# Sliding-window attention and a channel mix on one core: the tails of q and k in one transposition, q's part moved inside SBUF, the softmax division in two steps, multiplications that either of two engines may do, and new orders on all five engines

## The chip, the core and the metric

The kernel runs on one core of a Trainium2 chip. The core has TensorE (PE in the profile; its weight loads stand apart as PEld), VectorE (DVE), ScalarE (ACT), GpSimd (POOL) and SyncE (SP), and 16 DMA engines that its queues share. POOL's queue loads from HBM and turns float32 into bfloat16 on the way; SP's queue stores the output, copies inside SBUF and transposes by DMA. The metric is the device time of one launch in microseconds, the median of several runs. Before the change it is 231.72 us (three runs, 230.85 to 231.91).

## The reference

Batch 8, 8 heads, 576 tokens, head dimension 64; the channel mix has model width 512 and inner width 1024.

```python
# attention: causal, a window of 128 tokens, a linear bias by head
scores = scale * np.matmul(q, k.transpose(0, 1, 3, 2))
mask = (rel >= 0) & (rel < window)
scores = np.where(mask, scores + bias[None], -1000000000.0)
attn = np.exp(scores - np.max(scores, axis=-1, keepdims=True))
attn = attn / (np.sum(attn, axis=-1, keepdims=True) + 1e-09)
x = heads_side_by_side(np.matmul(attn, v))            # (8, 576, 512)
# channel mix; x_prev is x one token earlier, zero before the first
xk = mu_k * x + (1.0 - mu_k) * x_prev
xr = mu_r * x + (1.0 - mu_r) * x_prev
k = np.maximum(xk @ w_k, 0.0)
out = 1.0 / (1.0 + np.exp(-(xr @ w_r))) * (k * k @ w_v)
```

The middle lines are shortened: `heads_side_by_side` stands for a transposition and a reshape.

## The kernel before

**Pairs and batches.** The work on attention goes by pairs of heads: pair `it` is batch `it // 4`, heads `2 * (it % 4)` and the next, 32 pairs in all. Within a pair the 576 tokens are four blocks of 128 and a tail of 64. For the channel mix two batches make one group P of 1152 rows, four groups in all; a group's rows are cut into column chunks (`c0` is a chunk's first row), and its output into nine blocks of 128 rows.

**Steps and their names.** Every step has a name, and the engines' orders are lists of these names. For a pair: `tr` turns q and k of two pairs from "token by dimension" to "dimension by token" on VectorE (line 180; batches 0 and 1 do it on TensorE instead, `tq`, `tk`, and copy the result out of PSUM with `pq`, `pk`). `sh` copies the turned q inside SBUF, shifted by 32 partitions (line 196, SP's queue), because the scores read q of the next block at the same partitions as k. `score` multiplies k and q (lines 242 and 247; 229 in batches 0 and 1), `exp` is the exponential on ScalarE (line 263), `mask` multiplies by the banded bias on VectorE (line 271), `av` multiplies by v (line 287; a column of ones beside v gives the softmax's denominator), `norm` takes the reciprocal of that column (line 297) and multiplies by it (line 298), `ot` and `xt` transpose the result so that the model dimension lies on the partitions (TensorE and ScalarE, lines 306 and 317; from batch 4 on one DMA transposition on SP's queue, line 311). `dl` is x minus the token before (line 330), `ma` multiplies that by mu_k and by mu_r (line 336, two instructions), `xk` adds the token before (line 347). In batch 0 these steps come in two halves, columns 0 to 255 and 256 to 575.

For a group: `m1` is xk times w_k for one of eight slices of the inner width (line 359), `rl` the relu out of PSUM (ScalarE, line 365), `kk` its square (ScalarE, line 372, or VectorE, line 374: whichever list names it), `m3` is xr times w_r (line 381), `rs` its tanh (line 387), `m2a` and `m2` are the squares times w_v (line 396), `oo` joins both into the output (VectorE, line 402) and `st` stores it (SP's queue, line 408). `fill` are matrix products of zeros that TensorE does between other work in the first 31 us.

**The tails of q and k.** The last 64 tokens of a batch's q and k come by two loads on POOL's queue, `lts` (line 118; 64 KB each), each into partitions 64 to 95 of its half of a buffer that the turned tail of k later overwrites in part. `turn_tail` (line 188, steps `tl.b.0` and `tl.b.1`) then turns each with a VectorE operation of 32 partitions, into partitions 96 to 127, for batches 2 to 7: twelve operations. A batch's scores wait for both.

**Buffers.** Tiles of one kind rotate: four for the relu's output, three for the output, three for x's differences (`dl`), three for the scaled differences (`mb`), two PSUM tiles for scores and `av`, four PSUM banks for everything else.

**Order.** Five strings, one for each engine, fix the order of the steps on that engine word for word; an engine does them in that order and waits at each for what the step needs. The loop `plan` only interleaves the five lists and hands out rotating buffers in that order. SP's list mixes `sh`, `xt` and `st`: a step whose data are late holds up those behind it.

Of the kernel before, what the change touches and what calls it, by code (L numbers as in the profile page):

```python
# [16 lines left out]
def kernel(  # L17
# [12 lines left out]
    nc = tc.nc  # L30
# [29 lines left out]
    rlp = ctx.enter_context(tc.tile_pool(name="rlp", bufs=4))  # L60
    otp = ctx.enter_context(tc.tile_pool(name="otp", bufs=3))
# [15 lines left out]
    tl_buf = [kl.rearrange("p h c t -> p (h c t)").rearrange("p (i h c) -> p i h c", i=2, h=H)  # L77
              for kl in kl_buf]
# [9 lines left out]
    dl_buf = [cst.tile([128, S], BF16, name=f"dl{i}") for i in range(3)]  # L88
    mb_buf = [cst.tile([128, 2, S], BF16, name=f"mb{i}") for i in range(NMB)]
# [22 lines left out]
    def load_tail(b, i):  # L112
# [4 lines left out]
        else:  # L117
            nc.gpsimd.dma_start(
                out=tl_buf[b % 2][64:96, i],
# [65 lines left out]
    def turn_tail(b, i):  # L185
        dst = (words(kl_buf[b % 2], 128)[96:128, :, 0:64] if i else
               words(q2_buf[b % 2], 256)[96:128, :, 128:192])
        nc.vector.transpose(
            dst.rearrange("p h (c r) -> p h r c", r=2),
            tl_buf[b % 2][64:96, i].rearrange("p h c -> p (h c)").bitcast(FP32).rearrange(  # L190
                "p (h r d) -> p h r d", r=2, d=32))

# [98 lines left out]

    def norm(it, t0, t1):
        n = t1 - t0
        a5 = T.pop(("av", it, t0))[:, :, 0:n * W].rearrange("p h (t c) -> p h t c", c=W)
        rc = xup.tile([128, 2, NJ], FP32, tag="rc", name="rc")
        xu = T["xu", it, t0] = xup.tile([128, NJ, 2, D], BF16, tag="xu", name="xu")
        nc.vector.reciprocal(out=rc[:, :, 0:n], in_=a5[:, :, :, D])
        nc.vector.tensor_tensor(  # L298
            out=xu[:, t0:t1].rearrange("p t h d -> p h t d"), in0=a5[:, :, :, 0:D],
            in1=rc[:, :, 0:n, None].to_broadcast([128, 2, n, D]), op=ALU.mult)  # L300
# [28 lines left out]
    def delta(it, c0=0, c1=S):  # L329
        nc.vector.tensor_tensor(out=ring_of("dl", dl_buf, it, c0)[:, c0:c1], in0=x_of(it, c0, c1),  # L330
                                in1=x_of(it, c0 - 1, c1 - 1), op=ALU.subtract)

    def scaled(it, c0=0, c1=S):
        mb, g = ring_of("mb", mb_buf, it, c0), it % G
        for w in range(2):
            nc.vector.tensor_scalar(out=mb[:, w, c0:c1], in0=T["dl", it][:, c0:c1],  # L336
# [681 lines left out]
```

## Time and profile before

| | us |
|---|---|
| median of three runs | 231.72 |
| profiled execution | 231.78 |
| its span in the profile | 229.9 |
| TensorE busy in the span | 218.2 |
| VectorE busy | 190.4 |
| ScalarE busy | 172.7 |
| GpSimd busy | 76.4 |

The span runs from the first to the last instruction; 1.9 us of the profiled execution lie outside it. The granted TensorE clock was 1.00 in every stretch. A row of the groups by form names line, engine, operation, output and inputs, partitions by elements, count, then busy time in all and the mean duration of one in ns, then the idle time just before them. A row of the waits names who waited for whom, the total, how many times and the longest. A row of the stretches gives, for each engine, its busy time within the stretch.

### The profile page before, as it was taken

The page shows a single profiled execution, that of the slowest core. Times are in us where ns is not written, and L with a number is a line of the kernel's source. Part 1 is how long each engine was busy: PE and PEld are TensorE (multiplying, and loading weights), DVE is VectorE, ACT ScalarE, POOL GpSimd, SP SyncE. Part 2 cuts the span into 40 slices and gives each one's busy share as a digit, 9 for nine tenths or more (in the row PEclk, how much of TensorE's full clock was granted, in tenths as well). Part 3 has the DMA queues.
Part 4 walks back from the last instruction along what each step waited for, and adds up shares of the span by engine and source line. Part 5 has one row for each costly group of instructions (what it writes and reads, how often), then busy time and mean ns, then how long its engine had stood idle before and what let it go on. Part 6 is the DMA issues. An engine that isn't in the chain of part 4 may idle for free.

```text
span 229.9 us, 5654 instructions
## 1 busy us (share of the span) xinstructions
PE 218.2 (95%) x2226; PEld 128.1 (56%) x2261; DVE 190.4 (83%) x397; ACT 172.7 (75%) x326; POOL 76.4 (33%) x118
## 2 busy tenths in 40 slices
PE   7789989998999999999999999999999999999993
PEld 3446648755766555655566655556565465456541
DVE  7239999999899999999999999999989984761132
ACT  3968999996898997895699896868588668038810
POOL 8989864436565753271139100000000000000000
PEclk9999999999999999999999999999999999999999
DMA  5999999999999999999969996153422124240023
GB/s 112 164 145 157 175 157 201 209 172 182 228 199 185 182 210 199 155 134 208 114 128 112 220 141 146 33 165 128 91 80 74 48 56 120 99 152 26 0 98 130
DMA packets 83225, 31.82 MB, mean 138 GB/s; under 512 B 55032, under 2 KB 78592, under 8 KB 83200
## 3 DMA queue, kind: packets, MB, share of 16 engines
q0 software_dynamic: 61904, 16.52, 79.9%
q1 hardware_dynamic: 21296, 14.95, 25.8%
q8 instruction: 17, 0.28, 0.5%
q14 instruction: 8, 0.07, 0.1%
HBM read 33.56 MB, written 9.44 MB: 187 GB/s over the span
## 4 chain that ended last, share of the span: by engine, by line
PE 74%; DMA 10%; DVE 8%; POOL 3%; issue 1%; ACT 1%; SPq 1%; DVEq 0%; POOLq 0%
PE ps L359 25%; PE pv L396 22%; PE pr L381 11%; PE sa L287 6%; PE sa L242 4%; DMA qt<-qt 4%; DMA out_dram<-ot 3%; DMA vs<-in_v_dram 3%; DVE mb L336 2%; PE xp L306 1%; DVE xm L347 1%; PE sa L229 1%; DVE dl L330 1%; DVE xu L298 1%; PE sa L217 1%
## 5 line engine op out<-in xcount | busy, mean ns | idle before, releaser
L263 ACT ACTIVATE at<-sa 128x1024 bf16<-128x1024 f32 x64 | 64.0, 1031 | 13.7 <-PE sa L247 10.0
L359 PE MATMUL ps<-xm,wk_sb 128*128 128x256 bf16 (+2 forms) x412 | 70.4, 313 | 0.9 <-DVE xm L347 0.6
L396 PE MATMUL pv<-wv_sb,kk 128*128 128x512 bf16 x274 | 66.6, 379 | 0.8 <-issue 0.3
L365 ACT ACTIVATE rl<-ps 128x256 bf16<-128x256 f32 (+2 forms) x104 | 46.1, 474 | 14.0 <-PE ps L359 13.2
L359 PEld LDWEIGHTS <-wk_sb 128*128 128x128 bf16 x416 | 38.9, 98 | 22.5 <-issue 0.2
L396 PEld LDWEIGHTS <-kk 128*128 128x128 bf16 x288 | 26.9, 98 | 28.7
L372 ACT ACTIVATE kk<-rl 128x256 bf16<-128x256 bf16 (+2 forms) x79 | 38.4, 512 | 0.3
L271 DVE TENSOR_TENSOR at<-at,mask 128x1024 bf16<-128x1024 bf16 x56 | 36.9, 680 | 0.9 <-ACT at L263 0.8
L402 DVE SCALAR_TENSOR_TENSOR ot<-rs,pv 128x512 f32<-128x512 bf16 x36 | 24.4, 681 | 14.4 <-PE pv L396 10.5
L381 PE MATMUL pr<-wr_sb,xm 128*128 128x512 bf16 x131 | 35.2, 379 | 0.7
L99 POOL DMA_DIRECT2D vs<-in_v_dram x32 | 28.6, 902 | 20.1 <-PE sa L287 11.1
L387 ACT ACTIVATE rs<-pr 128x512 bf16<-128x512 f32 x36 | 21.3, 605 | 17.3 <-PE pr L381 17.1
L287 PEld LDWEIGHTS <-at 128*128 128x128 bf16 x576 | 21.6, 98 | 6.5 <-issue 1.0
L347 DVE TENSOR_TENSOR xm<-mb,xt 128x1152 bf16<-128x1152 bf16 (+3 forms) x40 | 24.4, 631 | 0.1
L298 DVE TENSOR_TENSOR xu<-sa,rc 128x640 bf16<-128x640 f32 x28 | 23.1, 824 | 1.0
L336 DVE TENSOR_SCALAR mb<-dl,mu_sb 128x576 bf16<-128x576 bf16 (+2 forms) x72 | 23.5, 386 | 0.2
L381 PEld LDWEIGHTS <-xm 128*128 128x128 bf16 x144 | 13.3, 98 | 12.3
L287 PE MATMUL sa<-vs,at 128*128 128x65 bf16 x448 | 18.8, 194 | 0.0
L242 PE MATMUL sa<-qt,kt 32*128 32x256 bf16 (+1 forms) x384 | 15.7, 266 | 1.2 <-DMA qt<-qt 0.7
L124 POOL DMA_DIRECT2D ql<-in_k_dram x15 | 11.7, 778 | 14.7 <-DVE kt L180 9.7
L374 DVE TENSOR_TENSOR kk<-rl 128x256 bf16<-128x256 bf16 (+2 forms) x25 | 8.0, 330 | 8.1 <-ACT rl L365 8.1
L330 DVE TENSOR_TENSOR dl<-xt 128x576 bf16<-128x576 bf16 (+2 forms) x36 | 14.6, 415 | 0.0
(72 smaller groups left out, 208.9 us busy)
## 6 DMA issues: line engine op xcount, KB each, us to landing
out_dram<-ot SPq DMA_DIRECT2D x36, 256.0 KB, 2.5
vs<-in_v_dram POOLq DMA_DIRECT2D x32, 128.0 KB, 8.3
ql<-in_k_dram POOLq DMA_DIRECT2D x15, 256.0 KB, 7.3
ql<-in_q_dram POOLq DMA_DIRECT2D x15, 256.0 KB, 7.6
qt<-qt SPq DMA_DIRECT2D x12, 192.0 KB, 6.8
wk_sb<-in_moe_w_k_dram POOLq DMA_DIRECT2D x2, 512.0 KB, 7.9
wv_sb<-in_moe_w_v_dram POOLq DMA_DIRECT2D x2, 512.0 KB, 13.2
tv<-in_v_dram POOLq DMA_DIRECT2D x8, 64.0 KB, 7.8
```

Source lines behind the costliest of these rows:

```text
L99: nc.gpsimd.dma_start(out=vs_buf[b % NLD][:, j, :, 0:D], in_=v[b, :, 128 * j:128 * j + 128, :].rearrange("h p d -> p h d"))
L263: nc.scalar.activation(out=to, in_=sa, func=AF.Exp, scale=float(scale))
L271: nc.vector.tensor_tensor(out=a, in0=a, in1=m, op=ALU.mult)
L287: nc.tensor.matmul(pa[:, hl, W * (t - t0):W * (t - t0) + W], lhsT=at[:, lo:lo + 128], rhs=vs[:, u, 2 * g + hl, :] if u < NF else tvb[:, 2 ...
L298: nc.vector.tensor_tensor(out=xu[:, t0:t1].rearrange("p t h d -> p h t d"), in0=a5[:, :, :, 0:D], in1=rc[:, :, 0:n, None].to_broadcast([12 ...
L336: nc.vector.tensor_scalar(out=mb[:, w, c0:c1], in0=T["dl", it][:, c0:c1], scalar1=mu_sb[:, NPO * w + g:NPO * w + g + 1], scalar2=None, op0 ...
L347: nc.vector.tensor_tensor(out=xm_buf[P % 2][:, w0:w1, o:o + c1 - c0], in0=T["mb", it][:, w0:w1, c0:c1], in1=x_of(it, c0 - 1, c1 - 1)[:, No ...
L359: nc.tensor.matmul(ps[:, 0:c1 - c0], lhsT=wk_sb[:, po, 128 * fo:128 * fo + 128], rhs=xk[:, po, c0:c1], start=(po == 0), stop=(po == NPO - 1))
L365: nc.scalar.activation(out=rl[:, 0:c1 - c0], in_=T.pop(("ps", P, c0, fo))[:, 0:c1 - c0], func=AF.Relu, scale=RELU_SCALE)
L372: nc.scalar.activation(out=out_, in_=in_, func=AF.Square)
L381: nc.tensor.matmul(pr, lhsT=T["xr", P][:, po, 128 * c:128 * c + 128], rhs=wr_sb[:, po], start=(po == 0), stop=(po == NPO - 1))
L396: nc.tensor.matmul(pv, lhsT=kk[:, fo, o:o + 128], rhs=wv_sb[:, fo], start=(fo == 0), stop=(fo == NFO - 1))
```

## The change

Six things change, and with them the order of the steps on every engine.

- **Tails.** Both loads go to one buffer, q in partitions 0 to 31 and k in 32 to 63, and one VectorE operation of 64 partitions turns both into partitions 64 to 127 (step `tl.b`, six operations instead of twelve). k's part lies there where the scores read it. q's part is copied from there by a new DMA on SP's queue, step `mt.b` (32 partitions of 8 times 256 bytes, 64 KB), and the scores wait for that copy.
- **Division.** `norm` is split in two steps with the same two instructions: `rc` (reciprocal) and `norm` (multiplication), so that other VectorE steps may stand between them.
- **Multiplications by mu.** `ma` and the new `mr` are the products with mu_k and mu_r, each a step of its own, and each may be on VectorE or on ScalarE, as the lists name them. 39 stand on VectorE and 29 on ScalarE (before: 72 on VectorE; in batch 0 the product with mu_r is no longer cut in halves). The difference, both products and their buffer are one rotating tile of three now, where there were three for differences and three for products.
- **Buffers.** Four for the output instead of three, three for the relu's output instead of four.
- **Squares and copies.** 45 of the 104 squares stand on VectorE instead of 25, and five of the eight copies `pk` instead of two.
- **Orders.** All five strings are new. TensorE has the same steps as before, the 14 `fill` among them.

```diff
-    rlp = ctx.enter_context(tc.tile_pool(name="rlp", bufs=4))
-    otp = ctx.enter_context(tc.tile_pool(name="otp", bufs=3))
+    rlp = ctx.enter_context(tc.tile_pool(name="rlp", bufs=3))
+    otp = ctx.enter_context(tc.tile_pool(name="otp", bufs=4))
...
-    tl_buf = [kl.rearrange("p h c t -> p (h c t)").rearrange("p (i h c) -> p i h c", i=2, h=H)
-              for kl in kl_buf]
+    tl_buf = [kl.rearrange("p h c t -> p (h c t)")[0:64, 0:1024].rearrange(
+        "p (h c) -> p h c", h=H) for kl in kl_buf]
...
-    dl_buf = [cst.tile([128, S], BF16, name=f"dl{i}") for i in range(3)]
-    mb_buf = [cst.tile([128, 2, S], BF16, name=f"mb{i}") for i in range(NMB)]
+    mb_buf = [cst.tile([128, 3, S], BF16, name=f"mb{i}") for i in range(NMB)]
...
-                out=tl_buf[b % 2][64:96, i],
+                out=tl_buf[b % 2][32 * i:32 * i + 32],
...
-    def turn_tail(b, i):
-        dst = (words(kl_buf[b % 2], 128)[96:128, :, 0:64] if i else
-               words(q2_buf[b % 2], 256)[96:128, :, 128:192])
+    def turn_tail(b):
         nc.vector.transpose(
-            dst.rearrange("p h (c r) -> p h r c", r=2),
-            tl_buf[b % 2][64:96, i].rearrange("p h c -> p (h c)").bitcast(FP32).rearrange(
+            words(kl_buf[b % 2], 128)[64:128, :, 0:64].rearrange("p h (c r) -> p h r c", r=2),
+            tl_buf[b % 2].rearrange("p h c -> p (h c)").bitcast(FP32).rearrange(
                 "p (h r d) -> p h r d", r=2, d=32))
+
+    def move_tail(b):
+        nc.sync.dma_start(out=words(q2_buf[b % 2], 256)[96:128, :, 128:192],
+                          in_=words(kl_buf[b % 2], 128)[64:96, :, 0:64])
...
+    def recip(it, t0, t1):
+        n = t1 - t0
+        a5 = T["av", it, t0] = T["av", it, t0][:, :, 0:n * W].rearrange(
+            "p h (t c) -> p h t c", c=W)
+        rc = T["rc", it, t0] = xup.tile([128, 2, NJ], FP32, tag="rc", name="rc")
+        T["xu", it, t0] = xup.tile([128, NJ, 2, D], BF16, tag="xu", name="xu")
+        nc.vector.reciprocal(out=rc[:, :, 0:n], in_=a5[:, :, :, D])
...
-    def scaled(it, c0=0, c1=S):
-        mb, g = ring_of("mb", mb_buf, it, c0), it % G
-        for w in range(2):
-            nc.vector.tensor_scalar(out=mb[:, w, c0:c1], in0=T["dl", it][:, c0:c1],
-                                    scalar1=mu_sb[:, NPO * w + g:NPO * w + g + 1], scalar2=None,
-                                    op0=ALU.mult)
+    def scaled(it, w, act, c0=0, c1=S):
+        mb, i = T["mb", it], NPO * w + it % G
+        mu = mu_sb[:, i:i + 1]
+        if act:
+            nc.scalar.activation(out=mb[:, w, c0:c1], in_=mb[:, 2, c0:c1], func=AF.Copy, scale=mu)
+        else:
+            nc.vector.tensor_scalar(out=mb[:, w, c0:c1], in0=mb[:, 2, c0:c1], scalar1=mu,
+                                    scalar2=None, op0=ALU.mult)
...
-            lq.0.0 lmu.0 lq.0.1 lmu.1 sh.2.0 sh.2.1 st.0.1 st.0.0 sh.3.0 st.0.2 sh.3.1
+            lq.0.0 lq.0.1 lmu.1 lmu.0 sh.2.0 mt.2 sh.2.1 mt.3 sh.3.0 sh.3.1 st.0.1 mt.4
...
-                for i in range(2):
-                    op(("tl", b, i), "DVE", 600, lambda i=i: turn_tail(b, i),
-                       [("lts", b, i)] + ([("clear",)] if i else []) + war, n)
+                op(("tl", b), "DVE", 640, lambda: turn_tail(b),
+                   [("lts", b, 0), ("lts", b, 1), ("clear",)] + war, n)
+                op(("mt", b), "SP", 60, lambda: move_tail(b), [("tl", b)], n, dma=300)
...
-            ready = [("tr", b, g // 2, 1), ("sh", b, g // 2), ("tl", b, 0), ("tl", b, 1)]
+            ready = [("tr", b, g // 2, 1), ("sh", b, g // 2), ("mt", b)]
```

Three places of the new orders follow, as the built programs have them. A row names line, operation, output and inputs, and the size of the output; the number after a name tells which buffer it is, and equal neighbours are counted in one row. Line numbers after the change are a few higher: the transposition of q and k is line 180 before and 179 after, that of the tails 188 and 185.

The first place is VectorE while batch 2 gets ready, between the division of batch 1 and its last `xk`. `qt` and `kt` are the turned q and k, `kl` the buffer of the tails. Before:

```order
L180 STREAM_TRANSPOSE kt_85<-ql_79 128x4x4x32
L297 RECIPROCAL rc<-sa 128x10
L298 TENSOR_TENSOR xu<-sa,rc 128x2x5x64
L330 TENSOR_TENSOR dl_99<-xt_95 128x576
L330 TENSOR_TENSOR dl_100<-xt_95 128x576
L336 TENSOR_SCALAR mb_102<-dl_99,mu_sb 128x576 x2
L330 TENSOR_TENSOR dl_98<-xt_95 128x576
L188 STREAM_TRANSPOSE kl_87<-kl_87 32x8x2x32
L347 TENSOR_TENSOR xm_96<-mb_102,xt_95 128x2x576
L374 TENSOR_TENSOR kk<-rl 128x256
L336 TENSOR_SCALAR mb_103<-dl_100,mu_sb 128x576 x2
L180 STREAM_TRANSPOSE qt_89<-ql_79 128x4x4x32
```

After:

```order
L179 STREAM_TRANSPOSE kt_85<-ql_79 128x4x4x32
L346 TENSOR_SCALAR mb_99<-mb_99,mu_sb 128x576 x2
L179 STREAM_TRANSPOSE qt_89<-ql_79 128x4x4x32
L337 TENSOR_TENSOR mb_98<-xt_95 128x576
L346 TENSOR_SCALAR mb_100<-mb_100,mu_sb 128x576
```

Between the transposition of k (first row) and the second one of q stood twelve instructions, and now stand two; the tail of batch 2 was turned earlier, in one operation.

The second place is SP's queue from the first copy inside SBUF on, `qt<-qt` being the shifted copy, `qt<-kl` the new copy of q's tail and `out_dram<-ot` a store. Before:

```order
L196 DMA qt_89<-qt_89 96x4x128 x2
L408 DMA out_dram<-ot 128x512 x2
L196 DMA qt_90<-qt_90 96x4x128
L408 DMA out_dram<-ot 128x512
L196 DMA qt_90<-qt_90 96x4x128
```

After:

```order
L197 DMA qt_89<-qt_89 96x4x128
L191 DMA qt_89<-kl_87 32x8x64
L197 DMA qt_89<-qt_89 96x4x128
L191 DMA qt_90<-kl_88 32x8x64
L197 DMA qt_90<-qt_90 96x4x128 x2
L417 DMA out_dram<-ot 128x512
```

The copies of the tails of batches 2 and 3 stand ahead of later shifted copies, and the first store now stands behind both shifted copies of batch 3.

The third place is ScalarE in the second column chunk of group 2 (384 wide), where `at<-sa` is the exponential, `mb<-mb,mu_sb` the multiplication by mu, `rl<-ps` the relu, `kk<-rl` the square and `rs<-pr` the tanh. Before:

```order
L365 ACTIVATE rl<-ps 128x384
L372 ACTIVATE kk<-rl 128x384
L365 ACTIVATE rl<-ps 128x384
L263 ACTIVATE at_84<-sa 128x2x2x256
L365 ACTIVATE rl<-ps 128x384 x3
L387 ACTIVATE rs<-pr 128x512
L372 ACTIVATE kk<-rl 128x384
```

After:

```order
L374 ACTIVATE rl<-ps 128x384 x5
L344 ACTIVATE mb_99<-mb_99,mu_sb 128x576
L396 ACTIVATE rs<-pr 128x512
L264 ACTIVATE at_84<-sa 128x2x2x256 x2
L396 ACTIVATE rs<-pr 128x512
```

Five relus now stand in a row with three buffers for them, and their squares are VectorE's.

324 lines of the change are left out of this document (168 added, 156 removed).

## The prediction

> **What bounds the kernel now.** I read the page first, then the busy time by stretches, then the waits, then the stretches around TensorE's waits. The page:
>
> ```profile
> PE 218.2 (95%) x2226; PEld 128.1 (56%) x2261; DVE 190.4 (83%) x397; ACT 172.7 (75%) x326; POOL 76.4 (33%) x118
> PE   7789989998999999999999999999999999999993
> DVE  7239999999899999999999999999989984761132
> ACT  3968999996898997895699896868588668038810
> ```
>
> TensorE is busy nearly everywhere after the first slices, but VectorE is as full until three quarters of the span. The stretches say how much each has left (columns: stretch, its length, then busy time of PE, PEld, DVE, ACT, POOL):
>
> ```profile
> 0.00:31.30 31.30, 27.24 (x345) 15.32 (x350) 21.12 (x74) 24.97 (x43) 27.29 (x54) 1.00 1.76 148
> 31.30:60.00 28.70, 27.22 (x333) 19.48 (x335) 27.69 (x55) 25.64 (x56) 16.15 (x21) 1.00 1.65 199
> 60.00:108.00 48.00, 47.38 (x511) 27.09 (x517) 47.25 (x84) 41.94 (x75) 24.02 (x32) 1.00 1.58 183
> 108.00:112.00 4.00, 3.67 (x50) 2.14 (x48) 3.36 (x6) 1.55 (x3) 0.00 (x0) 1.00 1.04 188
> 112.00:180.00 68.00, 67.01 (x718) 39.65 (x728) 65.88 (x128) 55.47 (x103) 8.94 (x11) 1.00 0.73 114
> 180.00:226.00 46.00, 45.64 (x284) 24.46 (x287) 24.44 (x55) 23.12 (x51) 0.00 (x0) 1.00 0.24 81
> ```
>
> 31.3 us is where the channel mix begins on TensorE, 226 where TensorE ends; the last 3.9 us are the last product and store. From 31.3 to 226 TensorE idles 1.48 + 0.62 + 0.33 + 0.99 + 0.36 = 3.78 us. The change takes no work off TensorE. So what it can win is within these 3.78 us and the first 31.3, where TensorE idles 4.06. The waits:
>
> ```profile
> PE sa L242 <- DMA qt<-qt: 0.7, 1, 0.7
> PE ps L359 <- DVE xm L347: 0.6, 1, 0.6
> PE sa L242 <- DVE xu L298: 0.3, 1, 0.3
> ```
>
> These are TensorE's waits of a known cause from 31.3 us on. The second is the channel mix's first product, which waits for `xk`; the first and the third are one place each:
>
> ```profile
> 46.79 1.10 DVE L180 STREAM_TRANSPOSE qt<-ql 128x512 f32<-128x512 f32 x1
> 47.91 8.06 DMA qt<-qt
> 56.11 0.40 PE L242 MATMUL sa<-qt,kt 32*128 32x256 bf16 x8 [0.70 <-DMA qt<-qt]
> ```
>
> Scores of pair 10 wait for the shifted q, whose copy took 8.06 us from the end of its transposition.
>
> ```profile
> 101.72 7.91 DMA out_dram<-ot
> 108.63 0.69 DVE L402 SCALAR_TENSOR_TENSOR ot<-rs,pv 128x512 f32<-128x512 bf16 x1 [0.16 <-DMA out_dram<-ot]
> 109.71 0.69 DVE L402 SCALAR_TENSOR_TENSOR ot<-rs,pv 128x512 f32<-128x512 bf16 x1 [0.39 <-DMA out_dram<-ot]
> 111.44 0.41 PE L242 MATMUL sa<-qt,kt 32*128 32x256 bf16 x8 [0.33 <-DVE xu L298]
> ```
>
> Here two outputs wait until a store has left one of the three output tiles; the division of pair 16 stands behind them on VectorE, and the scores of pair 20 wait for it to free a PSUM tile.
>
> **The change part by part.** The prices:
>
> ```profile
> L188 DVE STREAM_TRANSPOSE qt<-kl 32x512 f32<-32x512 f32 x6 | 4.2, 706 | 0.2
> L188 DVE STREAM_TRANSPOSE kl<-kl 32x512 f32<-32x512 f32 x6 | 4.2, 706 | 0.2
> L180 DVE STREAM_TRANSPOSE qt<-ql 128x512 f32<-128x512 f32 x12 | 13.2, 1102 | 0.0
> L336 DVE TENSOR_SCALAR mb<-dl,mu_sb 128x576 bf16<-128x576 bf16 x56 | 18.8, 385 | 0.2
> L336 DVE TENSOR_SCALAR mb<-dl,mu_sb 128x320 bf16<-128x320 bf16 x8 | 2.6, 362 | 0.0
> L336 DVE TENSOR_SCALAR mb<-dl,mu_sb 128x256 bf16<-128x256 bf16 x8 | 2.3, 419 | 0.0
> L374 DVE TENSOR_TENSOR kk<-rl 128x256 bf16<-128x256 bf16 x12 | 3.4, 282 | 0.5 <-ACT rl L365 0.5
> L374 DVE TENSOR_TENSOR kk<-rl 128x384 bf16<-128x384 bf16 x9 | 3.1, 354 | 7.6 <-ACT rl L365 7.6
> L374 DVE TENSOR_TENSOR kk<-rl 128x512 bf16<-128x512 bf16 x4 | 1.7, 418 | 0.0
> L372 ACT ACTIVATE kk<-rl 128x256 bf16<-128x256 bf16 x36 | 14.3, 430 | 0.1
> L372 ACT ACTIVATE kk<-rl 128x384 bf16<-128x384 bf16 x23 | 12.0, 533 | 0.1
> L372 ACT ACTIVATE kk<-rl 128x512 bf16<-128x512 bf16 x20 | 12.3, 635 | 0.1
> L129 DVE COPY qt<-tp 128x512 bf16<-128x512 bf16 x2 | 1.4, 690 | 3.2 <-PE tp L149 1.7 <-PE tp L154 1.5
> L132 ACT COPY qt<-tp 128x512 bf16<-128x512 bf16 x14 | 7.5, 607 | 0.5 <-PE tp L154 0.5
> ```
>
> *Tails.* Twelve operations of 0.706 us go, six of 64 partitions come. No row shows 64 partitions; at an equal 512 columns it lies between 0.706 (32 partitions) and 1.102 (128). A third of the way, as 64 lies between 32 and 128, is 0.84. VectorE saves 8.5 - 5.0 = 3.4 us (1.9 to 4.2).
>
> *Multiplications.* Busy time per instruction is 18.8/56 = 0.336 us, in halves 0.325 and 0.29. On VectorE 35 whole ones and four halves remain: 13.0 us against 23.7, a saving of 10.7. ScalarE gets 25 whole ones and four halves. It has no such row; the squares of 256 and 512 columns put 576 at 0.69 (0.64 to 0.75 allowed), halves at 0.43 and 0.48: 25 x 0.69 + 1.8 = 19.1 us more.
>
> *Squares and copies.* The lists have 18, 17 and 10 squares of 256, 384 and 512 columns on VectorE against 12, 9 and 4, which is 15.3 - 8.2 = 7.1 us more there and 6 x 0.430 + 8 x 0.533 + 6 x 0.635 = 10.7 less on ScalarE. Three copies add 2.1 on VectorE, and take 1.8 from ScalarE.
>
> VectorE: -3.4 - 10.7 + 7.1 + 2.1 = -4.9, 190.4 to 185.5 us. ScalarE: +19.1 - 10.7 - 1.8 = +6.6, 172.7 to 179.3. Neither is the path as such; what counts is TensorE's waits.
>
> *Term 1, the shifted q of batch 2.* From the division of pair 2 to the transposition at 46.79, VectorE now does less: one tail operation less (1.41 to 0.84), the four halves that go to ScalarE, in both products (2.45), the other halves of mu_r against three whole ones (1.2 - 1.0), and `dl`, both products and `xk` of pair 5, which now stand behind (0.4 + 0.7 + 0.7); more by a copy of 0.7, a copy of the mask of about 0.6 and two squares of 0.28. That is some 3.2 us less. It begins later by 1 to 1.5, since the reciprocal of pair 2 now waits behind more exponentials. The copy should land some 2 us earlier, and the wait of 0.70 goes: **-0.7** (0 if all of it is lost again).
>
> *Term 2, the fourth output tile.* The output at 109.71 no longer needs the store that has just left: **-0.4** (0 to -0.6, as VectorE idles 0.16 + 0.39 there and TensorE 0.33).
>
> *Term 3, a lighter VectorE.* Of the 1.97 us that TensorE idles in 60 to 108 and 112 to 226 I give a quarter to the 4.9 us less and to the reciprocals that no longer hold their multiplications: **-0.5** (0 to -2.0).
>
> *Term 4, the first 31.3 us.* The order of TensorE there is another: all scores of batch 1 and two of its `av` now precede the channel mix, about 2.4 us of work that stood behind. So its begin may come 2.4 us later at no cost. For it: VectorE's relief of 3.2. Against it: a load on GpSimd now precedes the distances from which ScalarE's masks are made, the reciprocal that waits, and w_k's loads, issued behind five loads of v. These look to be of one size, and I take **0** (-1.5 to +1.5).
>
> *At nothing.* The new copies: six issues on SP's queue, which stands waiting for VectorE most of the time.
>
> ```profile
> SPq L196 <- DVE qt L180: 59.4, 8, 32.7
> SPq L408 <- DVE ot L402: 62.7, 16, 13.8
> DMA to landing us min/median/max: 2.7/6.8/8.1
> ```
>
> The last row is that of the shifted copies. In five of six batches the tail's copy is issued ahead of one of that batch's own shifted copies, three times its size (64 against 192 KB), so the scores wait for that one anyway; in batch 5 it is issued right behind them. If it took 8.1 us and the cover were gone, each batch would lose up to the 0.7 that pair 10 lost. What waits behind it on SP are stores, and they now have a fourth tile. The split of the division adds no instruction.
>
> Sum: 231.78 - 0.7 - 0.4 - 0.5 + 0 = 230.2 us for the profiled execution, which lies 0.06 above the median: **230.1 us**.
>
> **The rivals.**
>
> *ScalarE becomes the bound (slower).* Its stretches, same columns as above:
>
> ```profile
> 20.00:50.00 30.00, 28.69 (x391) 20.06 (x396) 29.47 (x80) 28.97 (x61) 18.44 (x25) 1.00 1.68 180
> 60.00:100.00 40.00, 39.53 (x442) 23.21 (x447) 39.36 (x68) 36.13 (x67) 21.12 (x28) 1.00 1.58 182
> ACT rl L365 <- DVE kk L374: 0.6, 2, 0.4
> ```
>
> In 20 to 50 us it has 1.03 left. The lists put six multiplications there (3.2 us) and take a copy and, on balance, a square away (1.0): 1.2 too much. In 60 to 100 twelve whole ones come (8.3) and seven squares go (3.9): 36.13 + 4.4 = 40.5 in 40, 0.5 too much. With three relu tiles a relu also waits for VectorE's squares, as twice before with four; 20 more squares there at a third of the 0.3 of such a wait make 2 us, of which I count half. If ScalarE sets the pace, terms 1 to 3 don't count: 231.8 + 1.2 + 0.5 + 1.0 = 234.5; with half the relu waits hidden, 233.5. It decides once ScalarE idles less than about 1 us in 20 to 50. Against it: VectorE was at 29.47 of 30 there and cost TensorE little. The Trainium skill (ScalarE: Activation LUTs, Rules for kernel authors) tells to put multiplications on VectorE rather than ScalarE, since VectorE is faster per element; the trace agrees, 0.336 against some 0.69 us, and by that rule this rival should hold. The skill's Perfetto Trace Analysis (Optimizing Scalar/DVE Operations) allows the move where VectorE is saturated, which 29.47 of 30 shows.
>
> *The first 31.3 us eat the gain (no change).* The reciprocal of pair 2 stands ahead of a copy, the division of pair 0's second half and all its differences. If it waits 1.5 us and nothing makes that good, 230.1 + 1.5 = 231.6.
>
> *VectorE was the true bound (faster still).* If its 3.2 us by 46.8 reach TensorE in part, -1.5 in the beginning, and all of term 3's range: 231.7 - 0.7 - 0.4 - 2.0 - 1.5 = 227.1.
>
> *The move costs what it saves.* A 64-partition transposition of 1.10 us saves 1.9 instead of 3.4, and a late copy of q's tail costs 0.7 in each of six batches: 230.1 + 4.2 = 234.3. SP's waits above speak against it.
>
> **How the numbers follow.** Forecast 0.42 (229.0 to 231.0; I count a seventh of it as no change), VectorE as true bound 0.14, no change 0.23, ScalarE as bound 0.16, the late tail 0.05. A measurement tells from no change what is beyond 0.5%, 1.16 us: faster is below 230.56, slower above 232.88. Faster: 0.36 + 0.14 = 0.50; same: 0.06 + 0.23 = 0.29; slower: 0.21. The range runs from 227.6, near the third rival's end, to 233.5, the milder form of the first; the forecast's own is 229.0 to 231.0.
>
> **What would show it.** Right: no wait of the scores for the shifted copy, none of the output for a store, VectorE near 185.5 us busy and idling before 100, ScalarE near 179, TensorE idling under 2.5 us after its first channel-mix product. Wrong: long waits of relus for squares or for `mb`, a first channel-mix product later than 31.3 + 2.4 + 1 us, scores that wait for `qt<-kl`, or a tail operation above 1 us.

## The result, and the profile after

The changed kernel takes **242.81 us** (median of four, 240.64 to 243.49) against 231.68 (four runs, 230.85 to 231.91): ratio **1.0478, 95% interval 1.0436 to 1.0519**. 230.1 was forecast. Its profiled execution took 243.2 us, its span is 241.4. Here and below a ratio leaves out executions more than 1.5% above the fastest of the same kernel, and the kernel before was timed anew with each group of runs, so a ratio need not equal the quotient of the medians beside it.

The page of the changed kernel, busy times first, then the span in 40 slices of 6 us:

```profile
PE 223.7 (93%) x2226; PEld 129.6 (54%) x2261; DVE 181.5 (75%) x381; ACT 181.3 (75%) x332; POOL 76.9 (32%) x118
...
PE   8989889999999999999949699999999999999992
...
DVE  5346999989999789899397587999999858224032
...
PEclk9999999999999999999997979999999999999999
```

VectorE is 8.9 us lighter than before and still the kernel is 11 us longer. Counted from 1, TensorE has holes in slices 21 and 23 and VectorE in slices 20 to 25, and the granted clock dips in slices 22 and 24. The stretches of the changed kernel (columns as in the prediction: stretch, length, PE, PEld, DVE, ACT, POOL, granted clock, DMA share, GB/s) place the loss:

```profile
0.00:31.30 31.30, 27.39 (x344) 15.23 (x349) 19.57 (x59) 25.15 (x41) 29.26 (x57) 1.00 1.68 145
31.30:60.00 28.70, 27.46 (x323) 19.37 (x329) 27.73 (x65) 26.78 (x63) 14.68 (x20) 1.00 1.52 194
60.00:108.00 48.00, 46.67 (x535) 27.29 (x542) 44.55 (x80) 45.29 (x76) 21.81 (x29) 1.00 1.60 180
...
112.00:145.00 33.00, 27.30 (x256) 14.29 (x252) 23.77 (x44) 21.68 (x35) 8.64 (x11) 0.90 1.35 133
145.00:180.00 35.00, 34.47 (x372) 20.38 (x377) 32.36 (x65) 28.68 (x50) 0.00 (x0) 1.00 0.45 90
```

The same stretch of the kernel before:

```profile
112.00:145.00 33.00, 32.58 (x365) 19.79 (x369) 32.62 (x62) 28.32 (x56) 8.94 (x11) 1.00 1.18 141
```

TensorE does 256 matmuls there instead of 365. It idles 33.00 - 27.30 = 5.7 us, where it idled 0.4 before; its granted clock is 0.90 instead of 1.00. To see how late it is at each moment, I gave every step of TensorE's list its lower-quartile time in the two traces compared, and asked how much later than in the kernel before the same sum of work begins. In the changed kernel this lateness is -0.4 us at 30 us, 0.4 at 60, 1.8 at 100, 1.3 at 120, 5.8 at 130, 9.5 at 140, 11.2 at 145 and 11.0 at the end. **Nearly 10 of the 11 us are lost between 120 and 145 us.** Below, three numbers (at 120, at 145, at the end) stand for this.

Who waits between 80 and 146 us in the changed kernel (total, times, longest):

```profile
POOL ql L123 <- DVE kt L179: 12.4, 1, 12.4
DVE mb L337 <- DMA xt<-xu: 8.2, 3, 3.7
...
PE sa L243 <- DVE xu L303: 4.6, 3, 2.3
```

VectorE stands for x's transposition by DMA (`dl` waits for `xt`), and TensorE's scores stand for VectorE's division, which frees a PSUM tile. The chain of waits of the changed kernel (start, us, what) shows how the one makes the other:

```profile
92.74 7.97 DMA ql<-in_q_dram
...
107.65 11.51 DMA xt<-xu
...
125.83 0.83 DVE xu L303
...
127.25 8.72 DMA xt<-xu
...
136.37 0.83 DVE xu L303
...
137.25 0.37 PE sa L243 x5
```

x of pair 16 takes 11.5 us from its issue to its use, x of pair 20 takes 8.7. VectorE's own rows there:

```profile
114.68 0.82 DVE L303 TENSOR_TENSOR xu<-sa,rc 128x640 bf16<-128x640 f32 x1
119.19 0.46 DVE L337 TENSOR_TENSOR mb<-xt 128x576 bf16<-128x576 bf16 x1 [3.68 <-DMA xt<-xu]
...
132.92 0.21 DVE L299 RECIPROCAL rc<-sa 128x10 f32<-128x10 f32 x1
136.00 0.46 DVE L337 TENSOR_TENSOR mb<-xt 128x576 bf16<-128x576 bf16 x1 [2.86 <-DMA xt<-xu]
136.37 0.82 DVE L303 TENSOR_TENSOR xu<-sa,rc 128x640 bf16<-128x640 f32 x1
```

The last three are the point: the new list has the differences of pair 20 between the reciprocal and the multiplication of pair 21's division, and the scores of pair 24 wait for that multiplication. In the list before, the order there is `norm.21 dl.20`. And SP's queue of the changed kernel, where each step waits for its data in order:

```profile
112.68 0.55 SPq L417 DMA_DIRECT2D out_dram<-ot  x1
122.35 0.62 SPq L191 DMA_DIRECT2D qt<-kl  x1
123.03 0.61 SPq L197 DMA_DIRECT2D qt<-qt  x1
123.69 2.31 SPq L317 DMA_TRANSPOSE xt<-xu  x1
```

x of pair 19, divided at 115.5, leaves only at 123.7, behind the tail's copy and the first shifted copy of batch 6. These wait for VectorE, which itself waited 3.7 us for x of pair 16.

What shares the DMA engines with the transpositions: the view of the transfers from 105 to 140 us (40 slices, then the share of GpSimd's queue, then the transpositions with their median landing), of the changed kernel

```profile
DMA  9769999999996999999999999999999999984094
...
q0 software_dynamic: 12560, 2.62, 90.7%
...
xt<-xu SPq DMA_TRANSPOSE x6, 5.8
```

and of the kernel before:

```profile
DMA  9999999329017999039999399999999999893702
...
q0 software_dynamic: 10829, 2.23, 76.2%
...
xt<-xu SPq DMA_TRANSPOSE x6, 4.0
```

Before, the engines are lightly used for some 5 us from 111 us on, when the first transpositions run (slices of 3, 2, 9, 0 and 1 tenths, each 0.875 us). After, they are nearly full in every slice up to 135 us, and GpSimd's queue has 90.7%.

### The profile page after: what moved, and what is told of

The parts are those of the page before. It is cut to its first block, busy times and chain, and to the rows that moved or that the text cites. A ratio compares the mean times of both kernels' runs of the same rounds, so it can differ in the third digit from the quotient of the medians.

```text
span 241.4 us, 5640 instructions
## 1 busy us (share of the span) xinstructions
PE 223.7 (93%) x2226; PEld 129.6 (54%) x2261; DVE 181.5 (75%) x381; ACT 181.3 (75%) x332; POOL 76.9 (32%) x118
## 4 chain that ended last, share of the span: by engine, by line
PE 52%; DMA 23%; POOL 12%; DVE 9%; issue 2%; DVEq 0%; POOLq 0%
PE pv L405 19%; PE ps L368 17%; PE pr L390 9%; DMA xt<-xu 8%; DMA ql<-in_k_dram 6%; DMA wr_sb<-in_moe_w_r_dram 5%; POOL vs L98 3%; DMA ql<-in_q_dram 3%; POOL ql L123 3%; PE sa L288 3%; PE sa L243 3%; DVE xu L303 2%; DVE qt L179 2%; DVE kt L179 1%; POOL xm L113 1%
## 5 line engine op out<-in xcount | busy, mean ns | idle before, releaser
L368 PE MATMUL ps<-xm,wk_sb 128*128 128x256 bf16 (+2 forms) x412 | 71.9, 314 | 1.7 <-DVE ot L411 1.0
L405 PE MATMUL pv<-wv_sb,kk 128*128 128x512 bf16 x274 | 67.9, 387 | 1.1 <-issue 0.5
L405 PEld LDWEIGHTS <-kk 128*128 128x128 bf16 x288 | 27.4, 99 | 29.6 <-issue 2.2
L390 PE MATMUL pr<-wr_sb,xm 128*128 128x512 bf16 x133 | 35.9, 391 | 1.1 <-DMA wr_sb<-in_moe_w_r_dram 0.4
L411 DVE SCALAR_TENSOR_TENSOR ot<-rs,pv 128x512 f32<-128x512 bf16 x36 | 24.4, 682 | 15.4 <-PE pv L405 12.2
L381 ACT ACTIVATE kk<-rl 128x256 bf16<-128x256 bf16 (+2 forms) x59 | 29.3, 511 | 0.2
L383 DVE TENSOR_TENSOR kk<-rl 128x256 bf16<-128x256 bf16 (+2 forms) x45 | 14.7, 337 | 14.4 <-ACT rl L374 14.2
L303 DVE TENSOR_TENSOR xu<-sa,rc 128x640 bf16<-128x640 f32 x28 | 22.8, 816 | 0.4
L344 ACT ACTIVATE mb<-mb,mu_sb 128x576 bf16<-128x576 bf16 (+2 forms) x29 | 21.6, 758 | 0.2
L337 DVE TENSOR_TENSOR mb<-xt 128x576 bf16<-128x576 bf16 (+2 forms) x36 | 14.4, 413 | 8.9 <-DMA xt<-xu 8.6
L243 PE MATMUL sa<-qt,kt 32*128 32x256 bf16 (+1 forms) x384 | 16.5, 266 | 4.7 <-DVE xu L303 4.6
L243 PEld LDWEIGHTS <-kt 32*128 32x128 bf16 x384 | 8.6, 92 | 14.7 <-issue 6.4
```

The lines of the kernel that those rows point to most:

```text
L243: nc.tensor.matmul(T["sa", it, u // 2][:, u % 2, 256 * hl:256 * hl + n], lhsT=kt[r:r + 32, h, :, par], rhs=qt[r:r + 32, h, 0:n, par], star ...
L303: nc.vector.tensor_tensor(out=T["xu", it, t0][:, t0:t1].rearrange("p t h d -> p h t d"), in0=T.pop(("av", it, t0))[:, :, :, 0:D], in1=T.po ...
L368: nc.tensor.matmul(ps[:, 0:c1 - c0], lhsT=wk_sb[:, po, 128 * fo:128 * fo + 128], rhs=xk[:, po, c0:c1], start=(po == 0), stop=(po == NPO - 1))
L381: nc.scalar.activation(out=out_, in_=in_, func=AF.Square)
L390: nc.tensor.matmul(pr, lhsT=T["xr", P][:, po, 128 * c:128 * c + 128], rhs=wr_sb[:, po], start=(po == 0), stop=(po == NPO - 1))
L405: nc.tensor.matmul(pv, lhsT=kk[:, fo, o:o + 128], rhs=wv_sb[:, fo], start=(fo == 0), stop=(fo == NFO - 1))
```

## The experiments

The theory from this profile, **"late x"**: GpSimd's new order of loads brings the loads of batches 6 and 7 beside the transposing DMAs of pairs 16 to 20, these land late, and VectorE's new order puts the waits for them ahead of divisions that TensorE needs. Rivals: the **order on SP's queue** with the tail's copy in front; the **clock**, lowered for a cause of its own; **ScalarE** as the pace; the **merged tail** itself.

**1. Loads moved.** The diff is shortened; `lvs.6.2` and `lvs.6.4` also leave their later places.

```diff
  GpSimd: ... lql.6.1.0 lql.5.0.0
+ lvs.6.0 lvs.6.1 lvs.6.3 lvs.6.2 lvs.6.4
- lql.7.0.1 lql.7.1.0 lvs.6.0 lvs.6.1 lvs.6.3 lts.7.0
  lvs.7.2 lvs.7.1 lvs.7.0
+ lql.7.0.1 lql.7.1.0 lts.7.0
```

> The changed kernel, with GpSimd's list alone edited: the five loads of v of batch 6 are issued right behind the first k,q load that GpSimd last issues before its wait of 12.4 us (so at some 93 to 98 us instead of 107 to 125), and two loads of q and k and one tail of batch 7 go behind three loads of v of batch 7 (so after 114 us instead of 105.6). Nothing is loaded between about 98 and 114 us, where the transposing DMAs of pairs 16 to 18 run. Theory 'the transposing DMAs collide with GpSimd's loads': pair 16's differences no longer wait (11.5 us from issue to landing become 3 to 4), VectorE's wait for transposed x falls from 8.6 to under 4 us, TensorE's two idle times of 2.6 and 2.2 us and both stretches at half clock go or shrink: 232 to 236 us. Rival 'order on SP's queue, with the tail's copy in front': 240 to 243 us, as pair 19's transposition still stands behind the copies of batch 6. Rival 'ScalarE sets the pace': 242 to 243.

Measured: 243.47 us, ratio 1.0548 (1.0473 to 1.0623); lateness 1.4, 11.2, 11.0. No gain. Its waits between 80 and 150 us:

```profile
PE sa L243 <- DVE xu L303: 8.5, 2, 7.4
...
DVE mb L337 <- DMA xt<-xu: 8.3, 2, 4.7
```

The first half worked: pair 16's differences started on time at 115.5, and at 130 us the lateness was 1.9 instead of 5.8. But the loads now ran beside pairs 19 and 20 (12.2 us to use), and TensorE had one wait of 7.4 us instead of two. The collision moved; the theory's numbers were wrong for this edit, its mechanism was not refuted. The time lies nearest to what the two rivals gave, so this run alone rules out neither.

**2. Order on SP's queue.** `xt.19` from behind `st.1.0 mt.6 sh.6.0` to right behind `xt.18`.

> The changed kernel, with pair 19's transposing DMA moved on SP's queue from behind a store, the tail's copy and the first shifted copy of batch 6 to right behind pair 18's. It can then be issued at 115.5 us, when its division is done, instead of at 123.4. Theory 'collision with the loads': the waits for pairs 16 and 20 stay, and the 1.6 us for pair 19 goes: 239 to 242 us. Rival 'order on SP's queue': the wait of 2.2 us of TensorE and one of the stretches at half clock go with it, 234 to 237 us.

Measured: 242.1 us, 1.0482 (1.043 to 1.0535); 1.0, 9.8, 9.5. As "late x" expected, if 0.1 us above its range: pair 19 left at 115.2, and pair 20 became the wait (TensorE 4.6 us). SP's order is a link, not the cause.

**3. Tails apart.** The six merged operations and copies undone:

```diff
-            words(kl_buf[b % 2], 128)[64:128, :, 0:64].rearrange("p h (c r) -> p h r c", r=2),
+        for i in range(2):
+            dst = (words(kl_buf[b % 2], 128)[96:128, :, 0:64] if i else
+                   words(q2_buf[b % 2], 256)[96:128, :, 128:192])
...
-                op(("mt", b), "SP", 60, lambda: move_tail(b), [("tl", b)], n, dma=300)
```

> The changed kernel with one part undone: the tails of q and k are turned by two operations of 32 partitions again, q's part written straight to its place, and the six copies on SP's queue are gone; all other orders stay. Theory 'collision with the loads': the tail's copy is not what holds pair 19's transposition, as the shifted copy of batch 6 behind it waits for VectorE just as long; six operations of 0.71 us come back on VectorE: 242 to 245 us. Rival 'the moved tail costs it': pair 19 goes out earlier and the time falls to 233 to 237.

Measured: 240.83 us, 1.0419 (1.0357 to 1.0481), which cannot be told from the changed kernel and lies between the ranges of the two theories; 3.9, 11.6, 11.3, in an execution of 243.4 us that has one more stretch at half clock, at 33 us. The copy is not what holds pair 19: its transposition left at 121.0 us instead of 123.7, and VectorE's wait for x did not go.

**4. TensorE kept busy.** Eight matmuls of zeros ahead of `score.23`, eight ahead of `score.24`.

> The changed kernel with two groups of eight matmuls of 512 columns of zeros (1.7 us each) put into TensorE's list ahead of the scores of pairs 23 and 24, where it idles 2.6 and 2.2 us. They leave the computation as it is. Theory 'an idle TensorE is clocked at half afterwards': the stretches at 0.50 (128 to 131.5 and 138.3 to 141.6 us) go, and with them some 14 x 0.21 = 3.0 us: 239 to 240.5 us. Rival 'the clock was lowered for a cause of its own': the two stretches stay where they are, 243 to 244.

Measured: 239.74 us, 1.0395 (1.0322 to 1.0467); mean granted clock 0.999 instead of 0.984, both stretches at half clock gone. As expected; worth 3 us by the medians and 2 by the ratios, though the intervals overlap. The clock is a consequence of the idle times.

**5. Differences later on VectorE.**

```diff
- norm.19 dl.16 mask.20.1 ma.16 tr.6.0.0 tl.6 mr.16 oo.1.3 dl.17
+ norm.19 mask.20.1 tr.6.0.0 tl.6 tr.6.1.0 oo.1.3 dl.16 ma.16 mr.16 dl.17
- xk.17 dl.19 rc.21 dl.20 norm.21 kk.1.512.4 mask.23.1 kk.1.896.0 tr.7.1.0 xk.18 xk.19
+ xk.17 rc.21 norm.21 kk.1.512.4 mask.23.1 dl.19 kk.1.896.0 tr.7.1.0 xk.18 xk.19 dl.20
```

> The changed kernel with VectorE's list alone edited, around the waits for transposed x: pair 16's differences go behind two transpositions of batch 6 and an output, pair 19's behind the division of pair 21, a square and a mask, pair 20's from ahead of the division of pair 21 to behind the products of pair 19. Every DMA keeps its place. In the run with the loads moved, the three places became one wait of 7.4 us behind pair 20's transposing DMA, so neither loads nor SP's order alone is the cause. Theory 'VectorE's order puts a wait for a late DMA ahead of the division that frees a PSUM tile for the scores': the DMAs land as late as before (8 us and more), but VectorE's wait for them falls below 2 us, TensorE's waits of 2.6 and 2.2 us and the half clock go: 232 to 235 us. Rival 'the DMAs' lateness sets the pace wherever VectorE waits': the wait goes to the products of pairs 18 and 19 and to the channel mix of batch 4, 237 to 241. Rival 'ScalarE's load': 240 and more.

Measured: 235.57 us, 1.017 (1.0105 to 1.0235); 2.8, 5.9, 5.7 in a profiled execution of 238.0. **Seven of the eleven us come back with no DMA touched**, which is 0.6 us above the theory's range. Its waits:

```profile
ACT mb L344 <- DVE mb L337: 3.3, 1, 3.3
...
DVE kt L179 <- DMA ql<-in_k_dram: 2.7, 2, 1.4
...
DVE mb L337 <- DMA xt<-xu: 2.1, 3, 1.4
...
PE sa L243 <- DVE xu L303: 1.1, 1, 1.1
```

The transpositions landed as late as before (up to 11.4 us), but hardly anyone waited for them. What is left in the waits: a load of k for batch 4, issued at 77 and landed at 90 us, in front of pair 16's scores; and ScalarE's multiplication of pair 19, whose place was not moved.

**6. No late loads.** `load_v` does nothing for batches 6 and 7, `load_ql` nothing for batch 7.

> The changed kernel without the loads of v of batches 6 and 7 and of q and k of batch 7 (these batches compute with what the buffers held before, so their output is not meant): 14 of the loads that GpSimd issues from 105 to 126 us are gone, all lists stay. Theory 'the transposing DMAs are late because they share the DMA engines with these loads': pairs 16 to 20 land 2 to 4 us after their issue, as in the kernel before (2.7, 2.4, 2.8), VectorE's wait for them falls below 1.5 us: 231 to 234 us. Rival 'the transposing DMAs are slow behind one another or behind stores and copies on SP's queue': landings of 6 us and more stay, 238 us and more.

Measured: 233.94 us, 1.0114 (1.0065 to 1.0163); 1.0, 2.0, 1.3. **Eight to nine us come back with no order touched.** The same view of the transfers:

```profile
DMA  9899899999093000155288996100810000000009
...
q0 software_dynamic: 1072, 0.39, 17.2%
...
xt<-xu SPq DMA_TRANSPOSE x7, 3.3
```

VectorE waited 0.3 us for x, once. That the loads make x late is shown: pair 19's transposition landed in 3.9 us instead of 8.8. Pair 17's still took 7.5, more than the 2 to 4 expected, and nobody waited for it. That most of what lateness costs hangs on VectorE's order is shown by run 5.

**7. Both moves together** (1 and 5).

> The changed kernel with both edits that each moved the wait: the loads of the run with the loads moved, and VectorE's order of the run with the differences later. If loads and VectorE's order are the two halves of one cause, what the order alone left (scores of pair 16 0.9 to 1.4 us for a late load, scores of pair 25 some 1.7 us behind pair 19's differences) shrinks: 232 to 234.5 us. Rival 'the loads come back into the way of pair 19 and 20 as they did before': 236 and more.

Measured: 237.1 us, 1.0293 (1.0248 to 1.0338); 2.6, 5.2, 4.7. The rival's side: on top of run 5 the moved loads make it slower, by some 2.8 us (the two intervals lie apart).

**8. A fourth relu tile**, on run 5: `rlp` from 3 to 4.

> The run with the differences later, and a fourth relu tile beside four output tiles (room as in the run with the fourth output tile alone). The relus waited 4.3 us for VectorE's squares there, in five places. Theory 'ScalarE has slack behind the loads': 0 to 0.5 us. Rival of the prediction 'ScalarE becomes the bound, and three relu tiles add to it': 1 us or more faster.

Measured: 235.66 us, 1.0239 (1.0174 to 1.0305); 2.1, 6.3, 6.2. The relus' wait for squares is gone, and there is no gain: three relu tiles are not what costs.

**9. Multiplications back on VectorE**, on run 5: the 29 `ma` and `mr` of ScalarE's list, each behind its `dl`.

> The run with the differences later, and all 29 multiplications that went to ScalarE put back on VectorE, each right behind its differences. VectorE gets 25 x 0.376 + 4 x some 0.31 = 10.6 us more (181.5 to about 192), ScalarE 21.6 less (181.3 to about 160). Theory 'neither engine's load is what costs': within 1.5 us of the run that it starts from, 234 to 237. Rival 'ScalarE sets the pace': 2 us and more faster, 231 to 233.5. Rival 'VectorE's relief is what the change lives on': 2 to 4 us slower, 238 to 240.

Measured: 241.27 us, 1.0425 (1.0354 to 1.0496); 6.0, 7.6, 8.8. The last rival's direction, and above its range: in these orders VectorE's relief is worth 5.7 us. The Trainium skill (ScalarE: Activation LUTs, Rules for kernel authors) would have such products on VectorE; here, with VectorE busy 39.0 of the 40 us from 60 to 100 in this run, the measurement decides for ScalarE, although one takes 0.790 us there and 0.376 on VectorE.

**10 and 11. Loads by need.** From 64 us on all loads of batch 4, then of 5, 6 and 7; once with VectorE's order untouched, once with run 5's.

```diff
- lql.5.1.0 lvs.5.0 lql.5.0.1 lql.6.0.0 lql.4.0.1 lvs.5.1 ... lql.6.1.0 lql.5.0.0 lql.7.0.1 ...
+ lql.4.0.1 lql.4.1.1 lql.5.0.0 lql.5.0.1 lvs.4.0 lql.5.1.0 ... lvs.6.4 lql.7.0.0 ... lvs.7.3
```

> The changed kernel with GpSimd's list alone put in the order in which the loads are used, from 64 us on: all of batch 4, then 5, then 6, then 7. The load of batch 5 that came last at 92.5 us goes out near 70, the v of batch 6 near 95, so that behind 105 us only some q and k and the v of batch 7 remain. Theory 'loads that are late or lie beside the transposing DMAs': both shrink, but the v of batch 7 from 114 us still meets pairs 19 and 20: 234 to 238 us. Rival 'any load behind 105 us blocks VectorE as it stands': 240 to 243, as when five loads alone were moved. Rival 'the loads were the whole of it': 231 to 233.5.

Measured: 240.8 us, 1.0384 (1.0329 to 1.0438); 2.6, 7.6, 7.6. Inside the first rival's range: pairs 16 to 18 now met the q and k of batch 7, and VectorE still waited 3.2 us in one piece.

> The same order of the loads and VectorE's differences later. Theory 'what the order on VectorE left was late loads': scores of pair 16 no longer wait, 230.5 to 233.5 us. Rival 'something else in the new orders': 235 to 237, as with VectorE's order alone.

Measured: 237.12 us, 1.0268 (1.0215 to 1.032); 2.5, 4.1, 3.6. Pair 16's wait is gone (lateness 1.1 up to 110 us), but the time is the rival's, and no better than run 5's: late loads of batch 4 are not what run 5 left.

**12. No late loads and differences later** (5 and 6).

> The changed kernel without the loads of v of batches 6 and 7 and of q and k of batch 7 (the output of these batches is not meant), and with the differences later on VectorE. Theory 'with the loads gone nobody waits for x any more': the same as without the loads alone, 233 to 235 us, so that some 2.5 us lie elsewhere in the new orders. Rival 'VectorE's waits for x still cost': 231 to 232.5.

Measured: 235.75 us, 1.0211 (1.0162 to 1.0259); 2.6, 3.9, 3.4. This is above both ranges, and some 2 us slower than run 6 (the intervals just touch): where x is not late, moving the differences later gains nothing and seems to cost. So a part of the four us that run 5 left may be the price of its own order. With VectorE waiting 0.4 us for x, 2 to 4 us remain. 1.8 us of its lateness come at the scores of pair 16 (92 us), behind the late load of batch 4, which run 11 took away; 1.2 us are there by 60 us already. Which of the new orders makes these and the other small pieces **stays open**.

**13. The parts alone, in the kernel before.** Five runs. First the fourth output tile (`otp` from 3 to 4):

> The kernel before with a fourth output tile alone (for its 2 KB the scratch tile of the distances is laid into the first channel-mix buffer, which is written later). Term 2 of the prediction: the two outputs that waited 0.16 and 0.39 us for a store go ahead, 0.4 us faster: 231.3 against 231.7. Rival: the 0.33 us that TensorE idled there lie beside another wait, no difference. No theory expects a loss.

Measured: 230.56 against 231.02 us, 0.9975 (0.9945 to 1.0006): 0.6 us by the ratio, its sign not certain. The two outputs' waits for a store are gone.

Then that tile, and `tr.2.1.0` moved ahead of `tl.2.1`:

> The kernel before with a fourth output tile, and the transposition for pair 10's shifted copy moved ahead of the tail's and of three more operations on VectorE (2.1 us earlier). Terms 1 and 2 of the prediction: 0.7 + 0.4 = 1.1 us faster than before. Rival: the scores of pair 8 or the first products of batch 1 pay for it with 0.5 to 1 us, then no difference.

Measured: **230.18 against 231.08 us, 0.9961 (0.9937 to 0.9986)**. Terms 1 and 2 together are worth 0.9 us where the other orders stay; this version beats both kernels, the one before by 0.4%. No wait of TensorE for `qt` is left in its trace.

Then the merged tails with their copies, at the places the tails have in the lists before:

> The kernel before with the tails alone changed: one transposition of 64 partitions for a batch's two tails and a copy of q's part on SP's queue, at the places that the tails have in the lists of before. The transposition took 0.706 us in the changed kernel, so VectorE does 6 x 0.71 = 4.2 us less. Theory 'the changed parts are harmless, their new order isn't': 231 to 232 us, or up to 1 us less. Rival 'the moved tail is late': scores wait for the copy in several batches, 233 to 235 us.

Measured: 239.19 us, 1.0363 (1.0296 to 1.043), worse than both ranges. All of it at one place, the first scores of batch 2 (a wait, and two rows of the chain, of this run):

```profile
PE sa L244 <- DMA qt<-kl: 5.5, 1, 5.5
...
44.14 0.72 DVE kl L186
44.87 6.58 DMA qt<-kl
```

Lateness jumps from -0.5 to 6.8 us there, for the copy and 6.8 us of half clock, and stays. With batch 2's tail turned early:

> The kernel before with the tails alone changed, as in the run that lost 8 us, but batch 2's tail of k loaded some 12 us earlier, its one transposition at the place of the first of the two (about 30 us) and the copy ahead of the first shifted copy. There the scores of pair 8 waited 5.5 us for the copy (6.6 us from its transposition to landing) and TensorE ran at half clock behind it. Theory 'only the place of batch 2's copy cost': 230.5 to 231.5 us, level with before. Rival 'a merged tail costs in every batch': 233 and more.

Measured: 236.52 us, 1.0269 (1.0216 to 1.0321). The rival's side, but not by its mechanism alone, as my edit only moved the wait: VectorE stood 4.7 us for the load that I had put ahead of it (22.8 us), TensorE idled 3.4 us behind that, with 6.8 us at half clock, and the scores of pair 12 stood 0.9 us for the copy. At last all three parts, with the tails where nobody waits (batch 2's at 33 us, batch 3's right behind its first transposition):

> The kernel before with all three parts that the prediction priced: the fourth output tile, the earlier transposition for pair 10, and the merged tails with their copies, this time where nothing waits for them: batch 2's at 33 us behind its landed load, batch 3's right behind the first transposition of the batch, its copy behind the first shifted copy. VectorE does 4.2 us less. Theory 'the parts are worth a little, their new order cost': 229 to 230.5 us. Rival 'a copy between turning and scores costs wherever it is': 231.5 and more.

Measured: 231.77 against 231.12 us, 1.0028 (0.9998 to 1.0058): level with before, at the lower end of the rival's range, and by the two ratios some 1.5 us behind the version without merged tails. The part saves VectorE 4.2 us and earns nothing, even well placed. No score waits for the copy in this trace, so the rival's mechanism isn't seen, and where the 1.5 us go stays open.

## Why the prediction was wrong

- **The step that failed** is that the sum priced the new orders of GpSimd's loads and of VectorE's steps at nothing from 108 us on, with no term for VectorE's wait for x. I took it for granted that x's transposition would land as before. The rows of the kernel before (the trace has the landing of 13 of the 16):

```profile
L311 SPq DMA_TRANSPOSE xt<-xu x16: 1199/1219/1317, 111.5 to 189.6; - x16
...
DMA to landing us min/median/max: 2.6/2.6/7.4
```

- **What the runs showed in its place.** x of pairs 16 and 20 took 11.5 and 8.7 us from its issue to its use, VectorE waited 8.2 us for x between 80 and 146 us, and nearly 10 us were lost from 120 to 145. Without the late loads (run 6) eight to nine of the eleven us come back, with VectorE's differences later (run 5) seven. Both were to be seen beforehand: the lightly used DMA engines at 111 us, and `dl.20` placed ahead of `norm.21`.
- **The part "At nothing"** has a false sentence, "What waits behind it on SP are stores": transposing DMAs wait there too, and behind them VectorE and the scores. It was a link and not the cause: pair 19's transposition sent earlier (run 2) and the copies taken out (run 3) gained nothing clear of noise.
- **Term 3**, a lighter VectorE for -0.5, took load for time. VectorE did become lighter, 181.5 us against 185.5 foretold and 190.4 before, and run 9 shows that the relief is worth something in these orders, but 8.2 us of its free time between 112 and 145 us were waits for x.
- **Term 1** held in its mechanism: no wait of scores for `qt<-qt` is left, and the lateness falls from 1.3 at 50 us to 0.4 at 60. It had risen by more between 40 and 50, so nothing was won by 60.
- **Term 2** is of the right size in the kernel before (0.6 against 0.4, its sign not certain). In the changed kernel one output, at 80 us, still waited 1.4 us for a store, for all its fourth tile: that store stood behind copies of batches 3 and 4 on SP's queue, left only at 71.1 us and landed at 79.9.
- **Term 4** is right: TensorE was busy 27.39 us of the first 31.3, before 27.24. The first channel-mix product came at 35.2, 0.5 past the bound I had set; it cost nothing.
- **The copies of the tail** never held scores in the changed kernel, as foretold. But the bound of 0.7 us a batch was wrong by ten: taken out of their cover they cost 7.3 us in one place.

The prices, from the groups by form of the changed kernel:

```profile
L344 ACT ACTIVATE mb<-mb,mu_sb 128x576 bf16<-128x576 bf16 x25 | 19.3, 790 | 0.2
...
L346 DVE TENSOR_SCALAR mb<-mb,mu_sb 128x576 bf16<-128x576 bf16 x35 | 12.6, 376 | 0.1
...
L185 DVE STREAM_TRANSPOSE kl<-kl 64x512 f32<-64x512 f32 x6 | 4.2, 706 | 0.2
```

- The merged tail costs 0.706 us, no more than 32 partitions did; 0.84 was taken. ScalarE's product costs 0.790, outside the 0.64 to 0.75 that I allowed; its sum is 181.3 against 179.3.
- **Rivals.** ScalarE as the bound: relus waited 3.5 us for squares, but a fourth tile gave nothing and taking the products off ScalarE made it slower. VectorE as the true bound: no, it became lighter and the kernel slower. The first 31.3 us didn't eat the gain: the lateness is 0.4 us at 60. The late tail (0.05) had the right kind of mechanism, a DMA hop that leaves its cover, on the wrong DMA. A slip in the first rival's sum: with half of the relu waits that it counts hidden it comes to 234.0; 233.5 is what is left without any.

## What to carry to other kernels

When a change reorders queues, look in the trace of before for the transfers that are fast only because nothing else runs then, and in the new lists for the first instruction on an in-order engine that waits for one of them: what stands behind it is what the transfer's worst landing will cost. A DMA put in place of a short engine operation is priced by its landing under load (here 6.6 us for the copy of the tail, and up to 11.4 for a transposition), not by what it saves; put its consumer late or its producer early. Loads moved away from one transfer came to lie beside another here (runs 1 and 10), so first move the consumer that waits.

## What was unexpected

**The clock after a short idle.** Rows of the changed kernel by the microsecond (the third number from the end is the granted clock):

```profile
125.00:126.00 1.00, 0.00 (x0) 0.00 (x0) 0.97 (x5) 0.29 (x1) 0.74 (x2) 1.00 1.51 193
...
129.00:130.00 1.00, 1.00 (x4) 0.40 (x3) 1.00 (x4) 0.28 (x1) 0.00 (x0) 0.50 1.88 169
...
132.00:133.00 1.00, 1.00 (x21) 0.65 (x18) 0.46 (x2) 0.94 (x2) 0.00 (x0) 1.00 1.22 324
```

| run | TensorE idle, us | half clock |
|---|---|---|
| changed kernel | 124.4 to 126.7 (2.3) | 128.1 to 131.5 (3.4 us) |
| changed kernel | 135.3 to 137.2 (1.9) | 138.3 to 141.8 (3.4) |
| loads by need | 125.1 to 127.2 (2.1) | 128.2 to 131.6 (3.4) |
| tails apart | 132.8 to 136.2 (3.4) | 135.4 to 142.3 (6.8) |
| SP's order | 131.3 to 135.9 (4.6) | 136.4 to 139.8 (3.4) |
| loads moved | 129.9 to 137.3 (7.4) | 134.0 to 140.8 (6.8) |
| tails merged in the kernel before | 46.0 to 51.5 (5.5) | 49.1 to 55.9 (6.8) |
| the same, batch 2's tail early | 20.9 to 24.3 (3.4) | 22.9 to 29.7 (6.8) |
| tails apart | 31.6 to 33.0 (1.4) | 33.1 to 36.5 (3.4) |
| multiplications back | 109.0 to 110.7 (1.8) | none |
| SP's order | 122.9 to 124.3 (1.4) | none |

Every idle time of 1.9 us and more in these rows is followed by one or two stretches of 3.4 us at half rate, in four rows of eight after work has begun again; where all of it falls on work, 3.4 us at half rate cost 1.7 on top of the wait, by this arithmetic. Below that the length of one idle time doesn't decide: 1.8 and 1.4 us passed in two runs, and 1.4 us in the run with tails apart did not. There TensorE had more, shorter pauses too and was busy for 1.78 of the 3.45 us before the clock fell. What decides stays open. The Trainium skill (TensorE: Matmul & The Clock Gate, Part 1: The HAM clock gate) has a free-running window of about 3.4 us; the lengths agree. It gives an idle window of that length as what lowers the clock; here 1.9 us were enough, and once 1.4.

**A transposing DMA under load.** At best it landed in 2.6 us; beside GpSimd's loads it took up to 8.8 us in the changed kernel and 11.4 in run 5, and its issue on SP's queue took up to 3.1 us instead of 1.2. The rows of this line in run 5:

```profile
L317 SPq DMA_TRANSPOSE xt<-xu x16: 1201/1276/3092, 106.7 to 190.7; - x16
...
DMA to landing us min/median/max: 2.6/3.2/11.4
```
